# A spectral filter, soft mixture and gated layer on one core: the inverse basis multiplied straight into the spectrum, and expert weights loaded into the input's places

## Chip, core, metric

One core of one Trainium2 chip runs the whole kernel in one launch. The metric is device time in microseconds (us), the median of several runs. The kernel before takes 1540.72 us, the median of three runs (1538.58, 1540.72, 1543.03).

## What is computed

Three layers follow one another on 8 batches of 3072 tokens with 256 features each, all in float32.

```python
X = np.fft.rfft(x, axis=1)                       # x: (8, 3072, 256)
F = (filt_r + 1j * filt_i)[None, :, :]
y = np.fft.irfft(X * F, n=3072, axis=1).reshape(8 * 3072, 256)

logits = y @ phi                                 # 32 slots
d = softmax(logits, axis=0)                      # over all 24576 tokens
slot_input = d.T @ y                             # 32 x 256
slot_out = relu(slot_input @ w1[e]) @ w2[e]      # 8 experts, 4 slots each
z = softmax(logits, axis=1) @ slot_out

g = z @ w_gate
out = (silu(g) * (z @ w_val)) @ w_out            # 256 -> 1536 -> 256
```

## The kernel before

**First phase** (`phase1`). The kernel never transforms y back as a whole. It keeps the filtered spectrum in SBUF, since logits and slot inputs can both be had from it. The work is cut into 16 steps (8 batches, two halves `h` of 128 features), and a step into 6 units `u`. The loop over these 96 units writes the program in the order in which every engine runs it; nothing reorders it later.

- `s1_chunk` (lines 203 to 228) is the first stage of the Fourier transform: 4 chunks a step, each of 4 matmuls in four quadrants of the array (L217) into one PSUM tile `s`, a VectorE transpose to `sg` (L225), and a ScalarE copy to `b` (L234, in `spread`). It runs one step ahead of the units: in the usual plan one chunk in each of units 1 to 4.
- `s2_unit` (lines 239 to 271) is the second stage for one unit: 8 matmuls against the basis `fwd` (L248) into `X`, two VectorE products with the filter (P at L256, Q at L257), and two GpSimd combinations into `y` (L269, L271).
- `tr_unit` (lines 273 to 282) transposes `y` on TensorE against the identity (L279, 4 transposes a unit, two units later) and ScalarE copies the result (L281).
- `phi_pair` (lines 284 to 302), for every second unit, multiplies that by `phi` (L288) and gathers the slot logits' spectrum in `lts`.
- `chain` (lines 307 to 507) is a generator, one per batch, which `pump` advances by one step per unit while the next batch is under way. It transposes `lts` (L352), multiplies by the inverse basis `inv` (L362), transposes back (L372) and turns (L347) to the logits `lg`; takes the maximum (L397, L398), writes `lg` to memory (L402), forms exp(logit - max) (L420, L426), subtracts one (L430), transforms that forward again (L438, L450), puts the subtracted constant back at the zero frequency (L466), transposes (L471), and multiplies with `y` to the slot inputs of this batch (L481). Batch 6's chain is held back at step `HOLD` and interleaved with batch 7's behind the loop.
- `conv` (lines 558 to 597) reads 36 chunks of the three float64 weights `w_gate`, `w_val`, `w_out`, makes float32 out of their bits on VectorE (L584, L585, L591), ScalarE and GpSimd, and writes them back to memory. `first_weights` prepares the first batch's mixing weights. `aside` advances these two.

Loads are issued by SyncE, in program order: an issue that must wait for its place holds all issues behind it. `xp` holds two steps of x (16 KB of each partition for each), `bp` two steps of `b`, `sgp` the two `sg`. These, on the right side of SBUF, are given back behind the loop, and the first-layer expert weights `w1` (8 MB) go to their place (lines 714 to 718 and 758 to 762).

**Transition** (lines 731 to 871). `stage1` multiplies the slot inputs with `w1` (L783), `turn` transposes (L800), `stage2` multiplies with `w2` (L808, another 8 MB, in places that the first phase's tiles give back), and the result is multiplied with the gate and value weights (L843, L854).

**Second phase** (lines 940 to 1035). 576 items of 512 tokens by 128 hidden features: G and V (L959, L960), silu, product, split in two parts, and the output projection (L987, L991).

## Time and profile before

| | |
|---|---|
| median of three runs | 1540.72 us |
| the profiled execution | 1539.64 us, its span 1537.9 us |
| TensorE matmuls busy | 1449.9 us (94%) |
| VectorE busy | 1204.9 us (78%) |
| ScalarE busy | 955.1 us (62%) |
| GpSimd busy | 241.3 us (16%) |
| granted TensorE clock, mean | 0.991 |

The shares are averages over phases with different limits, so they are read by stage further down. "Busy" counts an engine from an instruction's start to its modelled end; a float32 matmul shows as two instructions, a transpose as one. "Idle before" gives the wait ahead of an instruction and what ended it. In the views by stretch the DMA share is the mean busy share of the core's 16 DMA engines.

### The profile page before, as it was taken

The page shows a single profiled execution, that of the slowest core. Times are in us where ns is not written, and L with a number is a line of the kernel's source. Part 1 is how long each engine was busy: PE and PEld are TensorE (multiplying, and loading weights), DVE is VectorE, ACT ScalarE, POOL GpSimd, SP SyncE. Part 2 cuts the span into 40 slices and gives each one's busy share as a digit, 9 for nine tenths or more (in the row PEclk, how much of TensorE's full clock was granted, in tenths as well). Part 3 has the DMA queues.
Part 4 walks back from the last instruction along what each step waited for, and adds up shares of the span by engine and source line. Part 5 has one row for each costly group of instructions (what it writes and reads, how often), then busy time and mean ns, then how long its engine had stood idle before and what let it go on. Part 6 is the DMA issues. An engine that isn't in the chain of part 4 may idle for free.

```text
span 1537.9 us, 26707 instructions
## 1 busy us (share of the span) xinstructions
PE 1449.9 (94%) x10282; PEld 1133.8 (74%) x10282; DVE 1204.9 (78%) x1976; ACT 955.1 (62%) x1808; POOL 241.3 (16%) x297
## 2 busy tenths in 40 slices
PE   3789998898869999999999999999999999999998
PEld 1455555555438888888888888888888888888887
DVE  3698899898328878887887788788778878877775
ACT  2365565564227666766766677677667667666665
POOL 1566555654010000000000000000000000000000
PEclk9999999999989999999999999999999999999999
DMA  9978678761990120121112013101301310120111
GB/s 193 189 132 147 115 132 142 124 117 56 366 279 25 35 68 19 29 69 27 27 35 71 16 28 69 30 23 35 72 15 29 69 35 18 35 62 14 28 29 28
DMA packets 90482, 116.53 MB, mean 76 GB/s; under 512 B 8657, under 2 KB 69970, under 8 KB 90034
## 3 DMA queue, kind: packets, MB, share of 16 engines
q1 hardware_dynamic: 88882, 111.15, 33.2%
q10 hardware_dynamic: 1216, 3.15, 1.1%
q8 instruction: 81, 1.33, 0.4%
q0 software_dynamic: 256, 0.52, 0.2%
q14 instruction: 47, 0.39, 0.1%
HBM read 68.13 MB, written 34.60 MB: 67 GB/s over the span
## 4 chain that ended last, share of the span: by engine, by line
PE 80%; DVE 11%; DMA 5%; issue 2%; ACT 1%; SPq 1%; POOL 0%; DVEq 0%; ACTq 0%; POOLq 0%
PE o L987 35%; PE o L991 18%; PE V L960 9%; PE G L959 9%; PE X L248 2%; DVE sg L225 2%; DVE P L256 2%; PE s L217 2%; DVE Q L257 2%; DMA fwd<-in_const_fwd_dram 2%; DMA raw<-in_moe_w_gate_dram 1%; PE T L279 1%; PE c L481 1%; DMA w<-in_moe_w_dram 1%; PE L L288 1%
## 5 line engine op out<-in xcount | busy, mean ns | idle before, releaser
L987 PE MATMUL o<-wo,hi 128*128 128x512 f32 x2304 | 831.1, 395 | 0.0
L991 PE MATMUL o<-wo,lo 128*128 128x256 f32 x2304 | 644.6, 280 | 0.2 <-DVE lo L976 0.2
L962 ACT ACTIVATE s<-G 128x512 f32<-128x512 f32 x576 | 344.7, 598 | 317.4 <-PE G L959 314.5
L968 DVE TENSOR_TENSOR h<-V,s 128x512 f32<-128x512 f32 x576 | 395.2, 686 | 168.9 <-ACT s L962 168.1
L987 PEld LDWEIGHTS o<-wo,hi 128*128 128x128 f32 x2304 | 432.0, 187 | 103.4
L991 PEld LDWEIGHTS o<-wo,lo 128*128 128x128 f32 x2304 | 433.6, 188 | 25.9 <-DVE lo L976 0.6
L976 DVE TENSOR_TENSOR lo<-h,hi 128x512 fp32r<-128x512 f32 x576 | 417.1, 724 | 0.1
L975 ACT CAST hi<-h 128x512 fp32r<-128x512 f32 x576 | 354.7, 616 | 12.5 <-DVE h L968 9.2
L960 PE MATMUL V<-c,v 128*128 128x512 f32 x576 | 227.4, 395 | 2.1 <-DVE h L968 1.8
L959 PE MATMUL G<-c,g 128*128 128x512 f32 x576 | 227.9, 396 | 0.0
L248 PEld LDWEIGHTS X<-b,fwd 128*64 128x64 f32 x1536 | 83.2, 138 | 67.9 <-issue 50.2
L959 PEld LDWEIGHTS G<-c,g 128*128 128x128 f32 x576 | 108.1, 188 | 25.6 <-issue 0.8
L234 ACT COPY b<-sg 128x768 f32<-128x768 f32 x64 | 58.7, 918 | 102.6 <-DVE sg L225 102.3
L225 DVE STREAM_TRANSPOSE sg<-s 128x1024 f32<-128x1024 f32 x64 | 78.9, 1236 | 47.9 <-PE s L217 47.9
L248 PE MATMUL X<-b,fwd 128*64 128x128 f32 x1536 | 106.3, 281 | 10.5 <-ACT b L234 5.0
L960 PEld LDWEIGHTS V<-c,v 128*128 128x128 f32 x576 | 108.6, 189 | 4.2 <-DVE h L968 2.9
L906 POOL TENSOR_TENSOR lg<-lg,mx 96x1024 f32<-96x1024 f32 x7 | 16.9, 2418 | 581.1 <-DVE mx L904 581.1
L217 PE MATMUL s<-x,csm 48*64 48x512 f32 x512 | 73.3, 628 | 34.2 <-DMA x<-in_x_dram 21.1
L1001 DVE TENSOR_TENSOR ot<-o,tmp 128x256 f32<-128x256 f32 x192 | 70.0, 423 | 39.5 <-ACT tmp L1000 39.5
L269 POOL TENSOR_TENSOR y<-P 128x256 f32<-128x256 f32 x96 | 70.2, 731 | 144.5 <-DVE P L256 144.5
L271 POOL TENSOR_TENSOR y<-Q 128x256 f32<-128x256 f32 x95 | 77.4, 815 | 0.9 <-DVE Q L259 0.8
L281 ACT COPY yt<-T 128x512 f32<-128x512 f32 x96 | 55.9, 582 | 30.4 <-PE T L279 29.9
(195 smaller groups left out, 1017.6 us busy)
## 6 DMA issues: line engine op xcount, KB each, us to landing
out_dram<-ot SPq DMA_DIRECT2D x192, 128.0 KB, 2.2
x<-in_x_dram SPq DMA_DIRECT2D x56, 384.0 KB, 8.2
w<-in_moe_w_dram SPq DMA_DIRECT2D x16, 1024.0 KB, 12.4
c<-ch SPq DMA_DIRECT2D x42, 128.0 KB, 2.4
c<-cl SPq DMA_DIRECT2D x42, 128.0 KB, 2.4
raw<-in_moe_w_gate_dram SPq DMA_DIRECT2D x12, 256.0 KB, 4.5
lgd<-lg SPq DMA_DIRECT2D x32, 96.0 KB, 6.9
raw<-in_moe_w_val_dram SPq DMA_DIRECT2D x12, 256.0 KB, 3.7
```

The lines of the kernel that those rows point to most:

```text
L217: pe.matmul(out=ps[64 * k:64 * k + 64, 16 * r:16 * r + 16, :], lhsT=s1t_sb[64 * r:64 * r + 48, :], rhs=xt[step][64 * r:64 * r + 48, k, :, ...
L225: dve.transpose(out=sg.rearrange("p j d k -> p d j k"), in_=ps.rearrange("p n d -> p d n"))
L248: pe.matmul(out=ps[par * 64:(par + 1) * 64, i, ri, :], lhsT=fwd[:, j, ri * 64:(ri + 1) * 64], rhs=bb[:, j, :],)
L271: eng.tensor_tensor(out=y[:, :, 1, :], in0=Q[:, :, 0, :], in1=Q[:, :, 1, :], op=ALU.add)
L959: pe.matmul(out=pg, lhsT=g4[c][:, fs], rhs=c4[b][:, q, G, :])
L960: pe.matmul(out=pv, lhsT=v4[c][:, fs], rhs=c4[b][:, q, G, :])
L962: act.activation(s, pg, AF.Silu)
L968: dve.tensor_tensor(out=h, in0=pv, in1=s, op=ALU.mult)
L975: act.copy(hi, h)
L976: dve.tensor_tensor(out=lo, in0=h, in1=hi, op=ALU.subtract)
L987: pe.matmul(out=a, lhsT=hi[:, ts], rhs=wo[f].rearrange("p k d -> p (k d)"), start=(f == 0), stop=(f == NF - 1), skip_group_check=True,)
L991: pe.matmul(out=a[:, D:2 * D], lhsT=lo[:, ts], rhs=wo[f][:, 0, :], start=False, stop=(f == NF - 1), skip_group_check=True,)
```

## The change

Five things are changed, all in the first phase and the transition.

1. `tr_unit` and its transposes go. `back_pair` takes their place: for two units together it multiplies the spectrum `y` (as the stationary operand, 64 rows at a time, the two halves of the array side by side) by the inverse basis `inv` (as the moving one): 16 matmuls into a PSUM tile of two banks, then one ScalarE copy of 1024 columns. The chain loses its first two steps (L352 as it was, and L362): it transposes `lts` once and turns it to logits. `inv` is needed from the first batch on, and is loaded ahead of the units. `phi_pair` now writes to the same PSUM tag as `back_pair`, which has one buffer.
2. The chain no longer subtracts one from the exponentials, nor puts the constant back. For all batches but the last, one reduction over both halves takes the place of two and their maximum.
3. Steps 2 and 3 (the second batch) get their x whole, in runs of 16 KB, in both x places, ahead of the units; step 4's load then has to wait until step 3's last chunk has read both. The first chunks of steps 3 and 4 move accordingly (`early`).
4. `w1` is loaded in pieces of 128 rows by 1024 columns into the places of x, `sg` and `b` as each comes free (behind units 83, 89, 90 and 95), so these pools stay until the transition has used them. The order of the `w2` loads changes.
5. The weight conversion starts four units later, and its last third (`w_out`) runs behind `first_weights`. The stores of `lg` of the last two batches are issued by ScalarE. `HOLD` is 5 in place of 8, in the shorter chain.

```diff
-HOLD = 8
+HOLD = 5
...
             def load_x(step, k):
                 b, h = divmod(step, 2)
-                if b >= NB:
+                if b >= NB or step == 3:
                     return
+                if step == 2:
+                    xt.setdefault(3, []).append(xp[k].tile([128, 16, D], F32, tag="x", name="x"))
+                    xt[2], ds = xt[3], slice(0, D)
+                else:
...
+            def expert_places(p, shape, tag, parts):
+                t = p.tile(shape, F32, tag=tag, name="w1")
+                for i, (e, d_) in enumerate(parts):
+                    w1s[e, d_] = t[:, i * FE:(i + 1) * FE] if len(shape) == 2 else t[:, i, :]
+                    nc.sync.dma_start(out=w1s[e, d_], in_=w1[e, 128 * d_:128 * d_ + 128, :])
...
-            def tr_unit(step, u):
...
-                        pe.transpose(out=ps[:, i, ri, :], in_=y[:, i, ri, :], identity=ident)
...
+            def back_pair(step, q):
+                b, h = divmod(step, 2)
+                ps = ps_t.tile([128, 2, 4, 128], F32, tag="T", name="T")
+                for g in range(4):
+                    y = yt[b, 2 * q + g // 2][:, g % 2]
                     for ri in range(2):
+                        for par in range(2):
+                            rows = slice(64 * par, 64 * par + 64)
+                            pe.matmul(
+                                out=ps[:, par, g, :],
+                                lhsT=y[rows, ri, h * 128:(h + 1) * 128],
+                                rhs=inv[rows, 2 * (4 * q + g) + ri, :],
+                                start=(ri == 0),
+                                stop=(ri == 1),
+                                tile_position=(64 * par, 0),
+                            )
+                t = ytp.tile([128, 2, 4, 128], F32, tag="yt", name="yt")
                 act.copy(t, ps)
...
             def phi_pair(step, q):
                 b, h = divmod(step, 2)
-                ps = ps_l.tile([128, 2, 2, 64], F32, tag="L", name="L")
+                ps = ps_t.tile([128, 2, 128], F32, tag="T", name="L")
...
-                lh = evac("lh", ps)
-                yield
-                ps = two()
-                for jj in range(NJ):
...
-                us = evac("us", ps)
-                yield
                 ps = small()
                 for k in range(6):
-                    pe.transpose(out=ps[:, k * 128:(k + 1) * 128], in_=col(us, k), identity=ident)
+                    pe.transpose(out=ps[:, k * 128:(k + 1) * 128], in_=lts[:, k // 2, k % 2], identity=ident)
...
-                for h in range(2):
-                    dve.tensor_scalar_add(dd[:, h], dd[:, h], -1.0)
...
-            side = [conv(), first_weights()]
+            side = [conv((0, 1)), first_weights(), conv((2,))]
...
+            early = [[], late, [[0], [1], [2], [3], [], []], [[], [], [0], [1], [2], [3]]]
...
+            at = [6 + p if p < 4 else 2 * p + 3 for p in range(len(units) // 2)]
+            behind = {a + 1: [p] for p, a in enumerate(at)}
...
             for i, (s, u) in enumerate(units):
-                if u in (0, 2):
+                if u in (0, 2) and s:
                     load_x(s + 2, u // 2)
-                if i == 6:
-                    nc.sync.dma_start(out=inv, in_=c_inv)
...
-                if i >= 8:
+                if i >= 12:
                     aside()
                 pump(1)
-                for c in plan[u] if s > 1 else late[u] if s else ():
+                for c in plan[u] if s > 3 else early[s][u] if s else ():
                     s1_chunk(s + 1, c)
...
+                if i == len(units) - 13:
+                    expert_places(xp[0], [128, 4, FE], "x", [(0, 0), (0, 1), (1, 0), (1, 1)])
+                if i == len(units) - 7:
+                    expert_places(xp[1], [128, 4, FE], "x", [(2, 0), (2, 1), (3, 0), (3, 1)])
+                if i == len(units) - 6:
+                    for d_ in range(2):
+                        expert_places(sgp, [128, FE], "sg", [(4, d_)])
+                    expert_places(bp[0], [128, 3, FE], "b", [(5, 0), (5, 1), (6, 0)])
...
-            cr.close()
-            for e in reversed(range(NEXP)):
-                w1s[e] = one([128, 2, FE], f"w1_{e}", c3, "right")
-            for e in range(4):
-                flat_load(w1s[e], w1[e], 128)
+            expert_places(bp[1], [128, 3, FE], "b", [(6, 1), (7, 0), (7, 1)])
...
-        for e in (4, 5):
-            flat_load(w1s[e], w1[e], 128)
-        flat_load(w2s[0], w2[0], 128)
-        for e in (6, 7):
-            flat_load(w1s[e], w1[e], 128)
         for e in (6, 7):
             flat_load(w2s[e], w2[e], 128)
         flat_load(wg, wd[0], 128)
-        for e in (1, 2, 3, 5, 4):
+        for e in (5, 0, 4, 1, 2, 3):
             flat_load(w2s[e], w2[e], 128)
         flat_load(wv, wd[1], 128)
```

**TensorE in a batch's stretch of the first phase.** The first rows are of the kernel before, three and a half units of the batch (X is a unit's second stage, T its transposes, L the product with phi, s the next step's first stage, c the chain; "x4" counts matmuls).

```order
L248 MATMUL X<-b,fwd 64x128 x8
L279 MATMUL T<-csm,y 128x128 x4
L288 MATMUL L<-yt,phi_sb 32x256 x4
L217 MATMUL s_1345<-x,csm 64x512 x4
L248 MATMUL X<-b,fwd 64x128 x8
L279 MATMUL T<-csm,y 128x128 x4
L352 MATMUL c<-csm,lts 128x128 x6
L217 MATMUL s_1391<-x,csm 64x512 x4
L248 MATMUL X<-b,fwd 64x128 x8
L279 MATMUL T<-csm,y 128x128 x4
L288 MATMUL L<-yt,phi_sb 32x256 x4
L362 MATMUL c<-inv,lha 32x128 x16
```

The same engine and place with the change (T is now the product with the inverse basis):

```order
L261 MATMUL X<-b,fwd 64x128 x8
L312 MATMUL L<-yt,phi_sb 32x256 x4
L230 MATMUL s_1320<-x,csm 64x512 x4
L261 MATMUL X<-b,fwd 64x128 x8
L295 MATMUL T<-inv,y 128x128 x16
L370 MATMUL c<-csm,lts 128x128 x6
L230 MATMUL s_1377<-x,csm 64x512 x4
L261 MATMUL X<-b,fwd 64x128 x8
L312 MATMUL L<-yt,phi_sb 32x256 x4
L387 MATMUL c<-t_1374,csm 64x512 x4
```

Units with 16 products and units with L now alternate, and the chain goes from its one transposition (L370) to the turned logits (L387) in the next unit.

**SyncE's issues behind the first batch's loads**, before (x of the second batch in pieces, `raw` the conversion's chunks, `wgd` its stores):

```order
L172 DMA x<-in_x_dram 48x16x128 x4
L570 DMA raw<-in_moe_w_gate_dram 128x512 x2
L172 DMA x<-in_x_dram 48x16x128 x2
L694 DMA inv<-in_const_inv_dram 128x3072
L172 DMA x<-in_x_dram 48x16x128 x2
L595 DMA wgd<-mn 128x256
```

and with the change:

```order
L645 DMA inv<-in_const_inv_dram 128x3072
L180 DMA x<-in_x_dram 48x4096 x4
L566 DMA raw<-in_moe_w_gate_dram 128x512 x2
L180 DMA x<-in_x_dram 48x16x128 x2
L591 DMA wgd<-mn 128x256
L566 DMA raw<-in_moe_w_gate_dram 128x512
```

The inverse basis and the second batch's whole x now stand ahead of the conversion. The third batch's first x load (the row with 48x16x128) stands ahead of the conversion's first store and of its third chunk.

## Rows read from the trace of the kernel before

**Rows 1.** Stretches, core 0: length, busy per engine, granted clock, DMA share, GB/s.
```profile
34.00:69.20 35.20, 25.50 (x300) 16.11 (x296) 24.62 (x41) 14.41 (x26) 20.48 (x29) 0.98 1.18 190
69.20:114.90 45.70, 40.83 (x481) 24.57 (x481) 40.80 (x68) 24.24 (x49) 24.45 (x33) 0.94 0.83 144
160.90:206.96 46.06, 41.75 (x534) 24.96 (x534) 42.12 (x71) 26.71 (x57) 27.02 (x37) 1.00 0.81 133
381.00:413.80 32.80, 24.43 (x336) 13.54 (x337) 16.17 (x41) 10.65 (x24) 3.06 (x5) 0.95 0.90 331
413.80:453.90 40.10, 27.20 (x236) 10.64 (x236) 5.57 (x9) 5.35 (x9) 0.00 (x0) 0.83 1.07 310
453.90:1537.90 1084.00, 1075.91 (x5764) 919.61 (x5760) 869.95 (x1414) 743.99 (x1385) 37.93 (x22) 1.00 0.16 38
```

**Rows 2.** Timeline of TensorE, one batch: the three waits, with the first-stage chunk.
```profile
188.61 0.27 PE L407 MATMUL c<-csm,cm 128*32 128x128 f32 x1 [1.01 <-DVE cm L398]
188.81 1.09 PE L217 MATMUL s<-x,csm 48*64 48x512 f32 x8
...
196.61 1.09 PE L217 MATMUL s<-x,csm 48*64 48x512 f32 x8 [1.57 <-DVE sg L225]
...
204.93 1.55 PE L450 MATMUL c<-fwd,bd 128*32 128x128 f32 x48 [1.04 <-DVE bd L347]
```

**Rows 3.** The same view: X, T and L of a unit, and the chain's transposes.
```profile
173.97 0.82 PE L352 MATMUL c<-csm,lts 128*128 128x128 f32 x6
...
182.72 1.09 PE L248 MATMUL X<-b,fwd 128*64 128x128 f32 x16
183.74 0.66 PE L279 MATMUL T<-csm,y 128*128 128x128 f32 x4
184.33 0.64 PE L288 MATMUL L<-yt,phi_sb 128*32 128x256 f32 x8
```

**Rows 4.** The chain of work that ended last, an inverse-basis step.
```profile
177.99 1.31 PE c L362 x48
```

**Rows 5.** Timeline of TensorE: two X in a row at the start; later units 6 and 12.
```profile
34.19 1.97 PE L248 MATMUL X<-b,fwd 128*64 128x128 f32 x32
...
47.09 1.09 PE L248 MATMUL X<-b,fwd 128*64 128x128 f32 x16
...
69.23 1.98 PE L248 MATMUL X<-b,fwd 128*64 128x128 f32 x16 [2.35 <-ACT b L234]
```

**Rows 6.** Timeline of TensorE's weight loads: the eight of one first-stage chunk.
```profile
188.81 0.21 PEld L217 LDWEIGHTS s<-x,csm 48*64 48x64 f32 x8
```

**Rows 7.** Groups of the first phase, shapes apart: weight loads of L217, copy of T.
```profile
L281 ACT COPY yt<-T 128x512 f32<-128x512 f32 x96 | 55.9, 582 | 30.4 <-PE T L279 29.9
...
L217 PEld LDWEIGHTS s<-x,csm 48*64 48x64 f32 x512 | 14.4, 134 | 61.0 <-DVE sg L225 27.3 <-issue 25.4 <-DMA x<-in_x_dram 4.8
```

**Rows 8.** Timeline of VectorE: the fourth unit's product; the subtraction of one.
```profile
44.14 0.69 DVE L256 TENSOR_TENSOR P<-X,ft 128x512 f32<-128x512 f32 x1 [4.12 <-issue]
...
198.15 1.83 DVE L430 TENSOR_SCALAR dd<-dd 128x512 f32<-128x512 f32 x2
```

**Rows 9.** Stretches again: whole x in flight; x in pieces in flight.
```profile
10.00:15.00 5.00, 0.00 (x0) 0.00 (x0) 0.00 (x0) 0.00 (x0) 0.00 (x0) 1.00 1.06 193
...
45.00:50.00 5.00, 4.52 (x62) 3.43 (x64) 4.48 (x8) 1.50 (x3) 4.82 (x8) 1.00 1.26 146
```

**Rows 10.** Timeline of TensorE: the last chain's start, and the transition's second stage.
```profile
387.36 1.03 PE L352 MATMUL cl<-csm,lts 128*128 128x128 f32 x6
...
390.91 0.66 PE L372 MATMUL c<-csm,usa 128*128 128x128 f32 x4 [0.33 <-ACT usa L334]
...
430.75 1.06 PE L808 MATMUL o<-w,ht 128*32 128x256 f32 x2 [8.03 <-DMA w<-in_moe_w_dram]
433.71 1.06 PE L808 MATMUL o<-w,ht 128*32 128x256 f32 x2 [1.90 <-DMA w<-in_moe_w_dram]
436.72 3.37 PE L808 MATMUL o<-w,ht 128*32 128x256 f32 x26 [1.95 <-DMA w<-in_moe_w_dram]
...
440.61 1.93 PE L808 MATMUL o<-w,ht 128*32 128x256 f32 x32
```

More of the change, by code (lines that the diff above doesn't have):

```diff
@@ L311, in two @@
                 def two(late=False):
-                    if late and b == NB - 2:
-                        return [p.tile([128, 512], F32, tag=t, name="cl") for p, t in ((ps_t, "T"), (ps_l, "L"))]
                     if not last:
-                        ps = small()
+                        ps = ps_t.tile([128, 1024], F32, tag="T", name="cl") if late and b == NB - 2 else small()
                         return [ps[:, 0:512], ps[:, 512:1024]]
@@ L324, in pair @@
                 def pair(name):
-                    if b == NB - 2 and name in ("dt", "dh"):
-                        return [ytp.tile([128, n], F32, tag="yt", name=name) for n in (512, 256)]
                     return [
@@ L382, in chain @@
                 else:
-                    lg = chp.tile([128, 2, E, 16], F32, tag="lg", name="lg")
-                    lg = [lg[:, h] for h in range(2)]
+                    both = chp.tile([128, 2, E, 16], F32, tag="lg", name="lg")
+                    lg = [both[:, h] for h in range(2)]
                 cm = chp.tile([128, 2, E], F32, tag="cm", name="cm")
@@ L426, in chain @@
                     act.activation(dd[:, h], dd[:, h], AF.Exp)
-                if not last:
-                    yield
-                for h in range(2):
-                    dve.tensor_scalar_add(dd[:, h], dd[:, h], -1.0)
                 yield
@@ L464, in chain @@
                     if q == 0:
[L465 to L467 removed]
+                        act.copy(sb_[:, b:b + 1], ps[0][0:32, 0:1])
                 yield
@@ L556, in flat, with conv @@
                 return a.rearrange("(p a) f -> p (a f)", p=128)
-            def conv():
+            def conv(kinds):
                 cw = 256
-                chunks = [(i, c) for i in range(3) for c in range(FF * D // 128 // cw)]
+                chunks = [(i, c) for i in kinds for c in range(FF * D // 128 // cw)]
                 raws = {}
@@ L648, in phase1 @@
                 load_filters(1)
+                nc.sync.dma_start(out=inv, in_=c_inv)
                 for step in range(2):
@@ L675, in pump @@
                 ready.clear()
+            at = [6 + p if p < 4 else 2 * p + 3 for p in range(len(units) // 2)]
+            behind = {a + 1: [p] for p, a in enumerate(at)}
             def tail_ops(i):
-                if 0 <= i - 2 < len(units):
-                    tr_unit(*units[i - 2])
-                if i - 4 >= 0 and i % 2 == 0 and i - 3 < len(units):
-                    s, u = units[i - 4]
-                    phi_pair(s, u // 2)
-                    if s % 2 == 1 and u == 4:
-                        ready.append((s // 2, chain(s // 2, s // 2 == NB - 1)))
+                for p in behind.get(i, ()):
+                    phi_pair(p // 3, p % 3)
+                    if p % 6 == 5:
+                        ready.append((p // 6, chain(p // 6, p // 6 == NB - 1)))
+                for p in (p for p in range(len(units) // 2) if at[p] == i):
+                    back_pair(p // 3, p % 3)
             def aside():
```

87 lines of the change are left out of this document (35 added, 52 removed).

## The prediction

> **What bounds the kernel now.** I read the time by stage first, because the shares on the page average over stages with different limits [rows 1]. From 453.9 us to the end the second phase keeps TensorE busy for 1075.9 of 1084.0 us, and the change touches none of its lines, so it costs nothing there. What can change is the 454 us ahead of it: the start (to unit 24, about 114.9), five even batches, the tail (to 413.8) and the transition (to 453.9).
>
> In an even batch (46.06 us) TensorE is busy for 41.75 us and VectorE for 42.12 [rows 1]: two engines near their limit, each of which now and then waits for the other. The timeline of TensorE shows where: 1.01 us for the maximum, 1.57 us for the transposes that free the only first-stage buffer, 1.04 us for the turn ahead of the forward transform [rows 2], 3.6 of the 4.3 us in which it stands. All three end with VectorE. At the start the DMA engines are full (share 1.18 from 34 to 69 us [rows 1]). In the transition, TensorE waits for expert weights at the second product, three times, 11.9 us in all [rows 10], and the granted clock averages 0.83 there [rows 1].
>
> **Even batches.** The new step has 16 matmuls of 128 columns for two units, shown as 32 instructions. Two X in a row take 1.97 us against 1.09 for one [rows 5]: 0.88 for sixteen instructions, 0.055 each, and 0.2 fixed. X also is 128 columns long and keeps two half arrays busy, split by columns where the new step splits by rows. At X's pace a pair costs 32 x 0.055 + 0.2 = 1.96 us. It takes the place of two T of 0.59 each (183.74 to 184.33 [rows 3]): +0.78 a pair, +4.7 a batch. The upper end is the pace of T, one transpose after another on the whole array: (0.59 - 0.2) / 4 = 0.10 each, so 3.4 us. I take 1.96, as the eight weight loads of a first-stage chunk, which go to four quarters of the array, end within 0.21 us [rows 6] where one of them takes 0.134 [rows 7]: loads into different row halves do run side by side. The Trainium skill, "TensorE: Matmul & The Clock Gate", section "LDWEIGHTS (loading the stationary operand)", speaks against the change: a load's time goes by its columns, and one of 32 rows takes as long as one of 128. One after another, by its formula (columns / 1.2 GHz, 107 ns for 128), the pair would take an estimated 3.6 us. The row above is what I go by.
>
> The chain loses the inverse basis step, 1.31 us [rows 4], and one of two groups of six transposes, 0.82 [rows 3]: -2.1. TensorE's work is then 41.75 + 4.7 - 2.1 = 44.35 us a batch. VectorE loses the subtraction, 1.83 us [rows 8], and two small instructions: 40.1 us. So TensorE becomes the only bound, and VectorE, 4 us behind it in work, should no longer make it wait much: between the logits' product and the maximum now lie a chunk, an X and often a full pair, about 4 us. I leave 0.7 us of waiting: 45.05 us, 1.0 less than now. From unit 24 to unit 86 are 62 / 12 = 5.2 batches: **-5 us**. Ends: no wait at all, -9; all 4.3 us kept, 48.65 us a batch, +13.5. ScalarE, with 26.7 of 46 us busy, hides its longer copy, and GpSimd's work stays.
>
> **The start.** Unit 6 starts at 47.1 and unit 12 at 69.2 [rows 5]. In units 6 to 9 there is now a pair in each, and L follows in the same single buffer, so each waits for the other's copy (0.58 us for half of T now [rows 7]). Unit 6: X 1.02 and T 1.96, with 0.5 for the inverse basis: 3.5. Units 7 and 8: 1.02 + 0.64 + 0.5 + 1.96, 4.1 each. Unit 9 the same plus a chunk of 1.02: 5.1. Unit 10: 2.7. Unit 11: X, T, two chunks and 1.3 between them: 6.3. Then the 2.35 us for the copy of b that unit 12 waits for today [rows 5]. Sum 28.1: unit 12 at 75.2. But unit 9's chunk needs the whole x of the second batch. It stands behind the filters, which the fourth unit's P waits for until 44.1 [rows 8], and behind the inverse basis (1.6 MB). At the 193 GB/s of the stretch in which the first batch's whole x is in flight [rows 9], 1.6 + 3.1 MB last 24 us: 65 to 68, where the chunk could run at 62.8. So unit 12 starts at about 78, +9.
>
> Behind it comes a wait that the change adds. Step 4's x goes where step 3's x still is until the end of unit 15, and SyncE holds its issue until then. Queued behind it are the conversion's first store and third chunk. That chunk's bytes follow 0.8 MB of x at about 146 GB/s [rows 9], 5.4 us, and land some 8 us after unit 15. VectorE meets the chunk in unit 16 and stands; TensorE has two X, an L and a pair to go before it needs the maximum behind that chunk: I put 5 us on the path. And as step 4's last chunk is made only in unit 23, unit 24 waits for b like unit 12: +2.4. From unit 12 to 24 that is 44.35 + 0.7 + 5 + 2.4 = 52.4 against 45.7 [rows 1]: +6.7. The start: **+15 us**; at least +7 (x in time, the chunk's wait covered), at most +18.
>
> **The tail.** The last chain starts with two steps fewer: 387.36 to 390.91 [rows 10], -3.5, and half of the subtraction, -0.5. Against that, the last pair with its longer copy adds 1.8, and the conversion's last third now falls on units 80 to 93, whose VectorE it had left: I put +1.2. Together **-1 us** (-5 to +3). The stores of the logits cost ScalarE issue time beside a wait for VectorE: nothing, 1 us if not hidden.
>
> **The transition.** w1 is in place before it. Behind unit 95 remain 1.6 MB of w1, 8.4 of w2 and 1.6 of the gate weights ahead of or among w2: 11.6 MB, where up to the second product there were 20 before. At 310 to 331 GB/s [rows 1] that is 35 to 37 us after 381, or 416 to 418; the second product starts near 422, a little earlier with the tail. So the three waits go, with the two pieces of 1.06 between them: 14.0 us. The clock too: 26 matmuls take 3.37 us behind the waits, 32 take 1.93 later [rows 10], so 1.8 more. That makes -15.8; I keep 1.3 for the last weights: **-14.5 us** (-16 to -6). Earlier loads run beside units 83 to 95, where the DMA engines are little used; their cover gone, they would show as waits of the first product.
>
> **Sum.** +15 - 5 - 1 - 14.5 = -5.5. The profiled execution took 1539.64 us (1.1 under the median): 1534.
>
> **Rivals.**
> *Weight loads of the two row halves don't overlap.* Then a pair takes 3.4 us, 1.44 more, on 48 pairs 69 us, nearly all on the path since TensorE is the bound: about 1600, slower. It decides early: from 2.1 us a pair on, the whole gain is gone. For it: no row here shows weights of 128 columns in two row halves; against it: rows 6. By the Trainium skill's page named above it would be 79 us more, an estimate. Chance 0.08.
> *TensorE keeps its waits*, because they come from the order of the program and not from VectorE's load: +13.5 for -5, so 1553, slower. For it: each wait ends with an instruction that stands in line behind other VectorE work. 0.13.
> *The start is nearly free* (+7): 1526. For it: the DMA engines carry 16 KB runs in place of 512 bytes. 0.25.
> *Loading w1 early doesn't do what it says*, since the waits shown are for w2, and w2's places come free no earlier; 6 us of wait stay: 1540, the same. 0.12.
>
> **How the numbers follow.** My forecast, 1534, has 0.42. About 0.3% (4.6 us) is what can be told from no change. Within the forecast's own spread I count 0.27 faster, 0.12 same, 0.03 slower; the free start is faster; the late w2 is mostly the same; the other two are slower (the kept waits with 0.02 as same). That gives 0.52, 0.25 and 0.23. The range reaches from the free start with no waits and 3 us more from the tail (1526 - 4 - 3 = 1519) to a start of 18 us with half of the waits kept (1534 + 3 + 9 = 1546), and leaves out the non-overlap and most of the kept waits.
>
> **What would show it.** Right: the pair's 32 instructions in about 2 us, an even batch near 45 us with TensorE over 97% busy, VectorE's wait for the third chunk behind unit 15, no wait of the second product over 1 us, w1 never waited for. Wrong: pairs of 3 us or more; a batch at 46 us or over; unit 24 before 122 us; waits for w2.

## The result, and the profile after

The changed kernel takes 1561.69 us, the median of four runs (1559.48 to 1567.1), beside 1541.88 us of the kernel before (four runs, 1538.58 to 1543.17): the ratio is 1.0137 with a 95% interval of 1.0103 to 1.0171. It is slower by some 20 us, and lies above the range of the prediction. The profiled span is 1562.1 us against 1537.9.

The start times of the first X of a unit (and of the first matmul of the transition's first product, and of the second phase), read from TensorE's timeline in us from the span's start, say where. The columns behind "after" are experiments below, by the first two characters of their labels.

| | before | after | r1 | r2 | r4 | f6 | g4 | g1 | h2 |
|---|---|---|---|---|---|---|---|---|---|
| unit 12 | 69.2 | 87.0 | 84.3 | 79.4 | 82.8 | 80.1 | 83.2 | 79.5 | 70.6 |
| unit 24 | 114.9 | 144.3 | 140.0 | 126.1 | 138.4 | 135.9 | 137.1 | 125.3 | 114.9 |
| unit 60 | 253.0 | 279.4 | 275.1 | 260.9 | 273.5 | 271.0 | 275.2 | 260.1 | 248.3 |
| unit 72 | 299.0 | 333.8 | 320.1 | 315.1 | 328.5 | 321.4 | 321.2 | 305.0 | 292.7 |
| unit 84 | 342.2 | 381.7 | 365.0 | 362.5 | 375.7 | 369.0 | 364.4 | 349.9 | 335.4 |
| unit 95 | 379.9 | 419.5 | 401.4 | 401.3 | 416.1 | 407.8 | 402.1 | 389.1 | 372.8 |
| transition | 413.8 | 454.1 | 440.5 | 433.6 | 447.1 | 451.1 | 435.0 | 422.3 | 408.6 |
| second phase | 453.9 | 478.2 | 493.0 | 457.8 | 485.3 | 475.2 | 476.8 | 446.4 | 438.0 |

To unit 24: +29.4. Units 24 to 60: 135.1 against 138.1, -3.0. Units 60 to 84: 102.3 against 89.2, **+13.1**. Unit 84 to the transition: +0.8. The transition: 24.1 against 40.1, -16.1. The sum, +24.2, is the difference of the spans. The medians differ by less: the profiled execution of after lies 2.2 us above the median of its four, and that of before 2.2 us below. Up to unit 24, after, r1, r4 and f6 run the same instructions, and the other three reach unit 24 at 135.9 to 140.0, so a start by itself varies by up to 8 us.

The stretches of after that answer to [rows 1]: start to unit 12, to unit 24, an even batch, the batches of units 60 to 72 and 72 to 84, and the transition (length, busy per engine, granted clock, DMA share, GB/s).

```profile
36.50:87.10 50.60, 35.15 (x422) 24.49 (x420) 22.54 (x35) 11.59 (x14) 16.82 (x24) 0.84 0.72 132
87.10:144.30 57.20, 48.53 (x625) 31.02 (x625) 38.44 (x65) 25.09 (x46) 27.23 (x36) 0.90 0.62 102
189.24:234.16 44.92, 43.94 (x627) 29.74 (x625) 38.70 (x66) 24.94 (x46) 27.63 (x37) 1.00 0.82 136
279.40:333.80 54.40, 46.90 (x627) 31.68 (x625) 40.33 (x64) 21.93 (x35) 24.12 (x30) 0.94 0.64 103
333.76:381.70 47.94, 44.76 (x626) 29.76 (x624) 36.58 (x66) 24.46 (x46) 26.16 (x37) 1.00 0.73 128
454.17:478.24 24.07, 23.06 (x237) 9.78 (x237) 5.64 (x9) 5.29 (x9) 0.00 (x0) 1.00 0.94 281
```

The even batch is as forecast: TensorE works 43.94 of 44.92 us, VectorE 38.70. The same work takes 54.40 us from unit 60 to 72 and 47.94 from 72 to 84, and the clock is down to 0.84 and 0.90 in the start, where before had 0.98 and 0.94. TensorE's timeline shows the places:

```profile
53.32 3.79 PE L295 MATMUL T<-inv,y 64*128 64x128 f32 x32 [3.83 <-DMA inv<-in_const_inv_dram]
...
72.86 1.07 PE L230 MATMUL s<-x,csm 48*64 48x512 f32 x2 [1.19 <-DMA x<-in_x_dram]
...
115.04 0.37 PE L409 MATMUL c<-csm,cm 128*32 128x128 f32 x1 [6.13 <-DVE cm L400]
...
207.42 2.06 PE L295 MATMUL T<-inv,y 64*128 64x128 f32 x32
209.40 0.29 PE L409 MATMUL c<-csm,cm 128*32 128x128 f32 x1
...
294.87 3.79 PE L295 MATMUL T<-inv,y 64*128 64x128 f32 x32 [5.49 <-DVE lts L324]
...
462.43 1.93 PE L807 MATMUL o<-w,ht 128*32 128x256 f32 x32
...
464.88 1.93 PE L807 MATMUL o<-w,ht 128*32 128x256 f32 x32
```

A product for two units (T) takes 2.0 us at the full clock (207.42 to 209.40) and 3.79 behind a wait, at the lower one. The maximum is no longer waited for (209.40, against 1.01 us in [rows 2]), nor is w2 (462.43, against [rows 10]). The two long waits, at 115 and 295 us, go back to VectorE, and from there to transfers:

```profile
113.27 0.29 DVE L580 TENSOR_SCALAR ex<-raw 128x256 int32<-128x256 int32 x1 [7.32 <-DMA raw<-in_moe_w_gate_dram]
...
292.20 1.00 DVE L607 TENSOR_REDUCE mx<-lgf 96x16 f32<-96x512 f32 x1 [5.06 <-DMA lgf<-lgd]
```

And SyncE's issues (time of issue, length) say why these are late:

```profile
38.94 3.01 SPq L180 DMA_DIRECT2D x<-in_x_dram  x4
42.64 1.24 SPq L566 DMA_DIRECT2D raw<-in_moe_w_gate_dram  x2
103.34 0.91 SPq L180 DMA_DIRECT2D x<-in_x_dram  x2
104.29 0.53 SPq L591 DMA_DIRECT2D wgd<-mn  x1
104.93 0.36 SPq L566 DMA_DIRECT2D raw<-in_moe_w_gate_dram  x1
...
283.27 0.40 SPq L603 DMA_DIRECT2D lgf<-lgd  x1
```

Nothing is issued from 43.9 to 103.3 us: step 4's x waits for its place, and the conversion's third chunk stands behind it, as predicted. The load of the first batch's logits (lgf) is issued at 283.27 and lands at 292.2, while `first_weights`, now in mid-phase at two steps a unit, wants it one unit behind.

### The profile page after: what moved, and what is told of

It is laid out like the page before. It is cut to its first block, busy times and chain, and to the rows that moved or that the text cites. A ratio compares the mean times of both kernels' runs of the same rounds, so it can differ in the third digit from the quotient of the medians.

```text
span 1562.1 us, 27951 instructions
## 1 busy us (share of the span) xinstructions
PE 1480.3 (95%) x11002; PEld 1178.0 (75%) x11002; DVE 1180.6 (76%) x1936; ACT 939.5 (60%) x1730; POOL 242.0 (15%) x297
## 4 chain that ended last, share of the span: by engine, by line
PE 83%; DVE 6%; DMA 6%; issue 1%; ACT 1%; POOL 1%; SPq 1%; DVEq 0%; ACTq 0%
PE o L986 34%; PE o L990 17%; PE V L959 9%; PE G L958 8%; PE T L295 4%; PE X L261 3%; PE s L230 2%; DMA x<-in_x_dram 2%; DVE sg L238 2%; DMA ft<-in_filt_r_dram 2%; PE c L477 1%; PE L L312 1%; DVE P L269 1%; DMA ft<-in_filt_i_dram 1%; DVE Q L270 1%
## 5 line engine op out<-in xcount | busy, mean ns | idle before, releaser
L261 PEld LDWEIGHTS X<-b,fwd 128*64 128x64 f32 x1536 | 85.1, 140 | 67.4 <-issue 53.6
L295 PE MATMUL T<-inv,y 64*128 64x128 f32 x1536 | 103.3, 286 | 15.0 <-DVE lts L324 8.4
L295 PEld LDWEIGHTS T<-inv,y 64*128 64x128 f32 x1536 | 94.1, 195 | 25.0 <-issue 12.8
L230 PE MATMUL s<-x,csm 48*64 48x512 f32 x512 | 77.1, 645 | 26.7 <-DMA x<-in_x_dram 24.3
```

The lines of the kernel that those rows point to most:

```text
L230: pe.matmul(out=ps[64 * k:64 * k + 64, 16 * r:16 * r + 16, :], lhsT=s1t_sb[64 * r:64 * r + 48, :], rhs=xt[step][k][64 * r:64 * r + 48, :, ...
L261: pe.matmul(out=ps[par * 64:(par + 1) * 64, i, ri, :], lhsT=fwd[:, j, ri * 64:(ri + 1) * 64], rhs=bb[:, j, :],)
L295: pe.matmul(out=ps[:, par, g, :], lhsT=y[rows, ri, h * 128:(h + 1) * 128], rhs=inv[rows, 2 * (4 * q + g) + ri, :], start=(ri == 0), stop=( ...
```

## The experiments

Ratios are to runs of the kernel before on the same chip (medians of 1540.3, 1543.3, 1542.3 and 1542.4 us in the four groups of runs: r, f, g and h). Times of different groups, and of after, are set against one another below as they are; as before's own median moves by 3 us among the groups, such a difference is uncertain by about as much.

### r1_order: the side work as before

```diff
-            side = [conv((0, 1)), first_weights(), conv((2,))]
+            side = [conv((0, 1, 2)), first_weights()]
...
-                if i == 10 or i >= 12:
+                if i == 10 or i >= 12 and (len(side) > 1 or i >= len(units) - 4):
```

> The changed kernel, but conversion and first batch's weights in the order and at the pace of before (all 36 chunks, then first_weights at one step a unit). Theory 1 (first_weights in mid-phase makes VectorE, and so TensorE, wait for its load of the logits): units 60 to 72 fall from 54.4 to about 46 us, units 72 to 86 by about 2.7, and some of it comes back in units 84 to 95; about 1551 us against 1561.7. Rival (these units are slow because of the pairs' own work or the rising VectorE load, whatever stands there): within 2 us of 1561.7.

Measured: 1578.17 us, ratio 1.0245 (1.0219 to 1.0271), slower still. Units 60 to 72 did fall to 44.9 us, and units 60 to 84 to 89.9 against 102.3. But the conversion starts four units later than in before, so the last step of `first_weights` falls behind the loop, where its VectorE instruction stands behind the last chains. Its store holds SyncE's queue, and w2 behind it; the waits of SyncE (us in total, times, longest) and TensorE's second product:

```profile
SPq L626 <- DVE ctf L624: 27.7, 2, 26.6
```
```profile
462.99 1.03 PE L807 MATMUL o<-w,ht 128*32 128x256 f32 x2 [14.13 <-DMA w<-in_moe_w_dram]
```

The theory held for the units that it named and failed in the time. So the mid-phase place is a cost, and the new order also had a use: it keeps the side work's end off w1 and w2.

### r2_pieces: the second batch's x in halves, as before

```diff
-                if step == 2:
-                    xt.setdefault(3, []).append(xp[k].tile([128, 16, D], F32, tag="x", name="x"))
...
-            load_x(2, 0)
-            load_x(2, 1)
...
-            early = [[], late, [[0], [1], [2], [3], [], []], [[], [], [0], [1], [2], [3]]]
+            early = [[], late, plan, plan]
```

> The changed kernel, but the second batch's x in halves of the features as before, and the first stage's chunks in the usual plan; the inverse basis still ahead of the units. Theory 2 (the start is lost to the order of transfers: 3.1 MB of x whole, on which unit 9's chunk waits and which hold the queue for step 4's x): unit 12 starts near 76 us in place of 87, unit 24 near 128 in place of 144; about 1546 us. Rival (the start is lost to the pairs and to the inverse basis, which is ahead in both): unit 24 falls by less than 5 us; about 1558 us.

Measured: 1544.24 us, ratio 1.0027 (1.0015 to 1.0039): 17.5 us below after. Unit 24 starts at 126.1. Units 60 to 72 still take 54.28. The theory of the start holds, and the size is right within 2 us.

### r3_unheld: step 4's x issued when its place is free

```diff
-                if u in (0, 2) and s:
-                    load_x(s + 2, u // 2)
+                if s and (u in (4, 5) if s == 2 else u in (0, 2)):
+                    load_x(s + 2, u // 2 if s != 2 else u - 4)
```

> The changed kernel, but step 4's x is issued in units 16 and 17, when its place is free, in place of units 12 and 14, so that it holds nothing behind it. Theory 2b (the held queue leaves the DMA engines idle from 74 to 103 us and costs the wait for the conversion's third chunk): unit 24 comes 6 to 8 us sooner, about 1555 us. Rival (the queue costs nothing, as the conversion would wait anyway for its first chunks behind x): within 2 us of 1561.7.

Measured: 1558.8 us, ratio 1.0113 (1.0093 to 1.0133), some 3 us below after, with intervals that overlap (after's is 1.0103 to 1.0171). Units 12 to 24 take 56.7 us against 57.2, and unit 24 starts at 140.7, within what the same code shows in after, r1, r4 and f6 (135.9 to 144.3); the 6 to 8 us that I had expected did not come. The wait for the chunk is gone, and another stands in its place. SyncE's issues, VectorE and TensorE of this kernel:

```profile
101.85 3.17 SPq L180 DMA_DIRECT2D x<-in_x_dram  x4
105.12 5.18 SPq L404 DMA_DIRECT2D lgd<-lg  x4
```
```profile
117.33 1.31 DVE L365 STREAM_TRANSPOSE bd<-c 128x512 f32<-128x512 f32 x2 [5.51 <-DMA lgd<-lg]
```
```profile
118.79 2.80 PE L448 MATMUL c<-fwd,bd 128*32 128x128 f32 x48 [5.28 <-DVE bd L365]
```

The stores of the logits now stand behind step 4's x, and `bd` takes the buffer that they free. Mending the held queue alone does not help: all of x, conversion and stores falls due in these units, and whichever is last is waited for.

### r4_w1late: w1 where before loaded it

```diff
-                if i == len(units) - 13:
-                    expert_places(xp[0], [128, 4, FE], "x", [(0, 0), (0, 1), (1, 0), (1, 1)])
...
+            cr.close()
...
+            for e in range(4):
+                flat_load(w1s[e], w1[e], 128)
```

> The changed kernel, but the w1 of the experts loaded where and in the order before loaded them, and w2 in the order of before. Theory 3 (early w1 takes the waits for w2 away and costs the first phase nothing): the transition is back at 40 us, 16 longer, units 83 to 95 unchanged; about 1577 us. Rival (the early loads collide with units 83 to 95): these units get 2 to 5 us shorter, about 1573 to 1575 us.

Measured: 1573.84 us, ratio 1.0212 (1.019 to 1.0234), 12.2 above after. The transition takes 38.2 us against 24.1, and units 84 to 95 do not get shorter (40.3 against 37.8). Early w1 is worth 14 us in the transition, and nothing shows that it costs the first phase anything in this order of the side work.

### f6_yields and f7_both: the load of the logits two steps earlier

```diff
                     nc.sync.dma_start(out=lg, in_=lgd[0][:, G])
-                    yield
-                    yield
+                    for _ in range(4):
+                        yield
```

> The changed kernel, but the first batch's weights wait four steps (two units) in place of two (one unit) behind the issue of their load of the logits; nothing else moves. Theory 1, sharpened by r1_order (units 60 to 72 were back at 44.9 us there, but the end of first_weights then stood behind the tail and held the queue): it is this one load, 8.9 us from issue to landing, that VectorE meets too early; its 5.06 us wait and TensorE's 5.49 us go, and the lower clock behind them: units 60 to 72 at 45 to 46 us, about 1553 us against 1561.7. Rival (the wait moves on to the second load or to another one behind it, as a wait moved in r3_unheld): units 60 to 84 shorter by less than 3 us, 1559 us or more.

Measured: 1563.55 us, ratio 1.0147 (1.0119 to 1.0174): no gain. Units 60 to 72 fell to 50.4 us, and units 60 to 84 from 102.3 to 98.0; VectorE still waits for the load, 2.4 us. But the conversion now ends two units later (95 in place of 93), and there its last chunk is issued behind nine loads of w1. VectorE meets it, and TensorE waits for VectorE:

```profile
399.95 4.68 SPq L187 DMA_DIRECT2D w<-in_moe_w_dram  x9
405.94 0.33 SPq L591 DMA_DIRECT2D wod<-mn  x1
407.25 0.33 SPq L566 DMA_DIRECT2D raw<-in_moe_w_out_dram  x1
```
```profile
416.35 0.29 DVE L580 TENSOR_SCALAR ex<-raw 128x256 int32<-128x256 int32 x1 [10.77 <-DMA raw<-in_moe_w_out_dram]
```
```profile
418.52 3.45 PE L295 MATMUL T<-inv,y 64*128 64x128 f32 x32 [9.63 <-DVE lts L324]
```

> The changed kernel with the second batch's x in halves of the features (as in r2_pieces) and the four steps behind the load of the logits. If the two costs are apart and add up: 1544.2 of r2_pieces less 8.5, about 1536 us, below before's 1540 to 1542. Rival (the waits are exchanged for one another): 1542 us or more.

Measured: 1551.65 us, ratio 1.0053 (1.0034 to 1.0071), where r2_pieces had 1.0027, with the same wait at the end (8.77 us). The rival held in f7_both. In f6_yields its time and its moved wait came, while units 60 to 84 got shorter by 4.3 us, more than the 3 that it allowed.

### f8_spread: the first products later

```diff
-            at = [6 + p if p < 4 else 2 * p + 3 for p in range(len(units) // 2)]
+            at = [9 + p if p < 7 else 2 * p + 3 for p in range(len(units) // 2)]
```

> As f7_both, but the first seven products with the inverse basis stand in units 9 to 15 in place of 6 to 11, 13 and 15. Theory (what is left of the start's loss, some 11 us by unit 24, is four products in a row, each waiting for the copy of the one ahead, the first two at the lower clock): unit 12 sooner by 4 us or more, unit 24 by about 3; about 3 us below f7_both. Rival (the work is merely moved, and TensorE is the bound up to unit 24): unit 24 within 1 us of f7_both.

Measured: 1563.96 us, ratio 1.0144 (1.0123 to 1.0164), 12 us above f7_both. My theory fell, and its rival too: it is worse. Unit 9 starts at 53.6 (f7_both: 60.1), but unit 16 at 108.9 (f7_both: 92.2). The products now stand among the chunks of steps 2 and 3, TensorE waits 0.6 to 1.5 us for ScalarE or VectorE ahead of each product from 66 to 106 us, and in the gaps the granted clock falls (the third column from the end of the stretches). These rows show where the time goes; what of it is the waits' and what the clock's was not taken apart:

```profile
60.00:70.00 10.00, 8.02 (x55) 5.22 (x57) 2.54 (x3) 1.26 (x2) 1.41 (x2) 0.55 0.94 141
70.00:80.00 10.00, 7.41 (x87) 3.98 (x84) 3.67 (x4) 4.01 (x5) 1.41 (x2) 0.94 0.01 4
80.00:90.00 10.00, 7.07 (x62) 5.38 (x60) 3.22 (x6) 1.32 (x3) 1.64 (x2) 0.57 0.57 80
```

### f10_w1late: f7_both without the early w1

The edit is that of r4_w1late on top of f7_both.

> As f7_both, but w1 loaded where before loaded it: of the five parts of the change only the product with the inverse basis, the shorter chain and the missing subtraction are left, with the small moves. By r4_w1late the early w1 is worth 12 to 14 us; so f7_both plus 12 to 14, about 1549 us, slower than before by 8. Rival (with the other two costs gone the product by itself wins): at or below before.

Measured: 1557.87 us, ratio 1.0096 (1.0078 to 1.0114), 6 above f7_both, where I had expected 12 to 14, and 9 above the forecast of 1549 us: the transition is 18.7 us longer, but the wait of 8.77 us goes with the w1 loads that caused it. The second product waits again:

```profile
449.46 1.06 PE L803 MATMUL o<-w,ht 128*32 128x256 f32 x2 [9.41 <-DMA w<-in_moe_w_dram]
```

### g1_three: three parts undone

r2_pieces, with the side work in before's order, at its pace and from unit 8 as in before. Against r2_pieces, order, pace and place of the side work thus change together:

```diff
-            side = [conv((0, 1)), first_weights(), conv((2,))]
+            side = [conv((0, 1, 2)), first_weights()]
...
-                if i >= 12:
+                if i >= 8:
                     aside()
...
-                if i == 10 or i >= 12:
+                if i == 4 or i >= 8 and (len(side) > 1 or i >= len(units) - 4):
                     aside()
```

> The changed kernel with three things as before: the second batch's x in halves of the features, the conversion from unit 8 and all of it ahead of first_weights, and first_weights at one step a unit. What stays of the change: the product with the inverse basis, the shorter chain, no subtraction, w1 into the places of x, sg and b. Theory (both losses come from the reordered side work and from the whole x, not from the product; in f6 and f7 and in r1_order the end of the side work ran into w1's loads or past the loop, and with four units more it no longer does): unit 24 near 124 to 126, units 24 to 84 at 45 us a batch, the tail as in r2_pieces, the transition 24 us: about 1530 us, faster than before by 10. Rival (side work at the old place meets w1's loads on SyncE's queue again): a wait of VectorE of 5 us or more behind unit 84, 1538 us or more.

Measured: **1531.09 us, ratio 0.993 (0.9914 to 0.9946)**, faster than before by 11 us and than after by 30. Its stretches (start, to unit 24, an even batch, transition) and TensorE in units 5 to 7:

```profile
34.70:79.50 44.80, 31.38 (x422) 23.34 (x418) 24.80 (x41) 13.58 (x20) 20.12 (x28) 0.92 1.03 169
79.50:125.30 45.80, 45.33 (x625) 30.63 (x625) 38.59 (x65) 23.91 (x45) 25.53 (x34) 0.96 0.76 126
170.26:215.18 44.92, 43.94 (x627) 29.73 (x625) 38.70 (x66) 24.95 (x46) 27.63 (x37) 1.00 0.79 136
...
422.33:446.41 24.08, 23.07 (x237) 9.78 (x237) 5.64 (x9) 5.29 (x9) 0.00 (x0) 1.00 0.90 268
```
```profile
46.84 3.68 PE L256 MATMUL X<-b,fwd 128*64 128x128 f32 x32 [5.08 <-DVE Q L265]
...
50.94 2.54 PE L290 MATMUL T<-inv,y 64*128 64x128 f32 x32 [0.43 <-DMA inv<-in_const_inv_dram]
...
55.80 2.06 PE L290 MATMUL T<-inv,y 64*128 64x128 f32 x32 [0.58 <-ACT lts L317]
```

Against before: start +10.4, units 24 to 84 -2.7, the tail +0.8, the transition -16.1; together -7.6 of the -7.9 between the spans.

### g2_minus_one: g1_three with the subtraction

```diff
                     act.activation(dd[:, h], dd[:, h], AF.Exp)
+                for h in range(2):
+                    dve.tensor_scalar_add(dd[:, h], dd[:, h], -1.0)
                 yield
...
-                        act.copy(sb_[:, b:b + 1], ps[0][0:32, 0:1])
+                        zero = dt_[0][0:32, 0:1]
+                        dve.tensor_scalar_add(zero, zero, float(SEQ))
+                        act.copy(sb_[:, b:b + 1], zero)
```

> As g1_three, but with the subtraction of one (two VectorE instructions a batch, 1.83 us) and the constant put back. Theory (VectorE is 6 us behind TensorE's work in a batch, so its work has cover): even batches within 0.3 us of g1_three, the time within 3 us. Rival (the chain's instructions stand in line on VectorE and each delays TensorE by its length): 1.8 us a batch, 12 us or so in all.

Measured: 1536.85 us (before: 0.9966, 0.9954 to 0.9977), 5.8 above g1_three; I had expected at most 3. A batch takes 45.39 us, 0.47 more (five of them 2.4), and unit 84 to the transition 3.9 more, where the last two chains run with little beside them. The 1.83 us of a batch are hidden to three quarters here, and not in the tail.

### g3_before_side: the side work's new order in the kernel before

```diff
-            side = [conv(), first_weights()]
+            side = [conv((0, 1)), first_weights(), conv((2,))]
...
-                if i == 4 or i >= 8 and (len(side) > 1 or i >= len(units) - 4):
+                if i == 4 or i >= 8:
```

> The kernel before with one part of the change: the conversion's last third behind first_weights, all at two steps a unit. Theory 1 (the order itself makes VectorE meet the load of the logits one unit behind its issue, whatever TensorE does): about 8 us are lost in the 12 units around first_weights (units 56 to 68), the time 1546 to 1550 us. Rival (it costs only where the products are, since TensorE has no slack there): within 2 us of before.

Measured: 1542.65 us, ratio 0.9999 (0.999 to 1.0009): the same. The wait is there, 3.28 us on VectorE and 4.05 on TensorE, but units 48 to 72 are only 3.0 us longer (95.0 against 92.1), and units 72 to 84, where part of the conversion now stands, another 1.8. This execution is the longest of its ten, and in the medians nothing of it is left:

```profile
250.29 1.00 DVE L611 TENSOR_REDUCE mx<-lgf 96x16 f32<-96x512 f32 x1 [3.28 <-DMA lgf<-lgd]
```
```profile
254.18 2.70 PE L450 MATMUL c<-fwd,bd 128*32 128x128 f32 x48 [4.05 <-DVE bd L347]
```

So the order costs 12.5 us in its units with the product, and by itself some 5 there, and nothing that can be told from the whole time. The rival's reason, that TensorE has no slack beside the products, fits; but the wait on VectorE is also shorter here (3.28 us against 5.06), so the reason isn't shown apart from that.

### g4_before_whole: the second batch's x whole in the kernel before

The edit makes `load_x`, the slices of x and the first chunks (`early`) those of the change; all else is before's.

```diff
+            load_x(2, 0)
+            load_x(2, 1)
+            early = [[], late, [[0], [1], [2], [3], [], []], [[], [], [0], [1], [2], [3]]]
...
-                if u in (0, 2):
+                if u in (0, 2) and s:
                     load_x(s + 2, u // 2)
```

> The kernel before with one part of the change: the second batch's x whole, ahead of the units, with the first chunks moved as the change moves them. Theory 2 (the whole x by itself costs the start): r2_pieces gave 17.5 us for undoing it in the changed kernel; without the inverse basis ahead of it x lands some 8 us sooner, so 8 to 12 us are lost by unit 24; about 1550 us. Rival (it costs only behind the inverse basis): unit 24 within 3 us of 114.9.

Measured: 1561.45 us, ratio 1.0123 (1.011 to 1.0136), 19 us slower by this part alone; unit 24 starts at 137.1, +22.2. The chain of waits, TensorE's timeline and VectorE's:

```profile
43.00 25.61 DMA x<-in_x_dram
```
```profile
68.65 1.96 PE L220 MATMUL s<-x,csm 48*64 48x512 f32 x2 [4.34 <-DMA x<-in_x_dram]
```
```profile
107.53 0.29 DVE L587 TENSOR_SCALAR ex<-raw 128x256 int32<-128x256 int32 x1 [6.93 <-DMA raw<-in_moe_w_gate_dram]
```

The product has no part in it: unit 9's chunk waits for all 256 features of x where its step needs 128, and the held queue brings the late chunk of the conversion with it.

### h1_before_w1 and h2_before_w1_nosub: without the product

The kernel before with the early w1, then also without the subtraction. The first edit is `expert_places` and its four calls as in the change, its order of w2, and

```diff
-            cr.close()
-            for e in reversed(range(NEXP)):
...
+            expert_places(bp[1], [128, 3, FE], "b", [(6, 1), (7, 0), (7, 1)])
...
-                        nc.sync.dma_start(
+                        (nc.scalar if b >= NB - 2 else nc.sync).dma_start(
```

> The kernel before with one part of the change: w1 into the places of x, sg and b, the change's order of the w2 loads, and the last two batches' stores of the logits issued by ScalarE. Theory 3 (the early w1 is worth its 12 to 14 us by itself): about 1528 us. Rival (in before, the longer chain's tail and the side work's end at unit 95 leave it less): 1533 us or more.

Measured: 1531.43 us, ratio 0.9928 (0.9911 to 0.9944): 11 us by the early w1 (with its order of w2 and the stores on ScalarE), near the theory. The transition takes 28.8 us here, 11.4 less than in before, where after has 16.1 less. The other 4.7 us go with a wait for w2 and the lower clock behind it, which this kernel and the next still show. SyncE holds w2's loads until a slot-input product of the last chains (L487) has read the place: 10.2 us here, where the longest such wait in g1_three is 3.4 us. SyncE's wait in this kernel (total, times, longest), and TensorE's second product:

```profile
SPq L128 <- PE cl L487: 10.2, 1, 10.2
```
```profile
427.38 3.54 PE L813 MATMUL o<-w,ht 128*32 128x256 f32 x26 [2.33 <-DMA w<-in_moe_w_dram]
```

So the last 5 us of the transition's gain come with the rest of the change, under which w2's places are free sooner; the product, the shorter chain and the smaller `HOLD` were not tried apart in this.

```diff
-                    dve.tensor_scalar_add(dd[:, h], dd[:, h], -1.0)
...
-                        zero = dt_[0][0:32, 0:1]
-                        dve.tensor_scalar_add(zero, zero, float(SEQ))
-                        act.copy(sb_[:, b:b + 1], zero)
+                        act.copy(sb_[:, b:b + 1], ps[0][0:32, 0:1])
```

> As h1_before_w1, and without the subtraction of one. Theory 4 (the product with the inverse basis by itself is a loss of some 7 us: 10 at the start, and half of the gain of the batches is the missing subtraction's): about 1524 us, faster than g1_three by 7. Rival (the product is what makes VectorE's work cheap; with the transposes the engines wait for one another as before): 1531 us or more, no faster than g1_three.

Measured: **1520.02 us, ratio 0.9856 (0.984 to 0.9873)**, the fastest of all: 22 us below before, 11 below g1_three, 42 below after. The missing subtraction alone is worth 11.4 us here by the medians. The two profiled executions differ by 5.8 us only, as that of h1_before_w1 is the shortest of its four and this one, at 1524.45 us, the longest; units 24 to 84 take 6.8 us less, and where the rest of the 11.4 lies isn't shown. An even batch of this kernel, in the stretches:

```profile
159.58:203.96 44.38, 41.23 (x535) 24.85 (x535) 40.32 (x68) 26.60 (x57) 26.81 (x37) 1.00 0.77 138
```

With the transposes TensorE still waits for 3.15 us of a batch, and the batch is 0.54 us shorter than g1_three's, where it works 43.94 and waits for 1.

### h3_before_inv: only the inverse basis ahead

```diff
+                nc.sync.dma_start(out=inv, in_=c_inv)
                 for step in range(2):
...
-                if i == 6:
-                    nc.sync.dma_start(out=inv, in_=c_inv)
```

> The kernel before with one part of the change: the inverse basis loaded ahead of the units in place of unit 6. Theory 4 (the start's remaining +10 are TensorE's four products in units 6 to 9, with copies and the lower clock): unit 24 within 2 us of 114.9, 1542 us. Rival (it is the 1.6 MB ahead of the second batch's x): unit 24 later by 5 us or more, 1547 us.

Measured: 1545.15 us, ratio 1.0019 (1.0009 to 1.0028): 2.7 us by the medians. In the profiled execution, at 1549.5 us the longest of its ten, unit 24 comes 7.2 us later, and unit 9's chunk waits for x:

```profile
62.36 1.96 PE L217 MATMUL s<-x,csm 48*64 48x512 f32 x2 [1.22 <-DMA x<-in_x_dram]
```

The rival holds in the profile, and the medians lie between the two: of the 10 us that g1_three loses at the start some 3 to 7 are the transfer's, an estimate, and what is left I put down to the products by subtraction.

## Why the prediction was wrong

**The start, +15, was the first failed step**: it measured +29.4 in the profile, and +21 to +29 over the four kernels with the same code up to unit 24, past its upper end of +18. The mechanisms were right and their terms too small. "1.6 + 3.1 MB last 24 us: 65 to 68" rested on 193 GB/s, but x landed at 72.9, and while it was in flight all transfers together moved 173 GB/s:

```profile
43.90:73.00 29.10, 19.62 (x239) 15.39 (x240) 9.21 (x15) 5.16 (x7) 9.81 (x14) 0.82 0.95 173
```

And no term stood for the clock, which fell behind these waits, so that T took 3.79 us for 2.0. I charged the whole x with some 10 us (3 to unit 12, 5 for the third chunk, 2.4 for b). Undoing it gave 17.5 (r2_pieces), doing it alone cost 19 (g4_before_whole). What the product and the early inverse basis cost the start without it is +10.4 (g1_three), where my working had +6.

**The second failed step was one left out.** "The conversion's last third now falls on units 80 to 93" looked at where the conversion goes and not at what takes its place: `first_weights` in units 60 to 70, at twice the pace, with a load that it meets one unit after the issue. The new order cost 12.5 us there (units 60 to 84: 102.3 in after, 89.9 in r1_order). How much of that is this one load's stays open: a further unit of distance took back 4.3 us (f6_yields), with 2.4 us of VectorE's wait left. Before's rows could not show the wait; that VectorE would meet the load sooner stood in the order of the program, and I had costed VectorE's work there, not its waits.

**The even batches, -5, were right per batch, for the wrong reason, and wrong in number.** The product took 2.0 us for 1.96, the batch 44.9 for 45.05. But I let VectorE's relief pay for the product. Taken apart, the relief alone brings the batch to 44.4 (h2_before_w1_nosub), and the product then puts back what it adds to TensorE: the 2.6 us of work that I had worked out eat TensorE's last waits and 0.5 more. And I multiplied one batch's gain by 5.2, though before's batch of units 72 to 84 already took 43.15 us, as its conversion ended there (in unit 79); with the product it takes 44.9. This stretch in before:

```profile
299.02:342.17 43.15, 41.23 (x534) 24.83 (x534) 39.21 (x66) 24.68 (x51) 25.31 (x35) 1.00 0.71 126
```

So g1_three gains 2.7 where I had 5, and h2 gains 6.8.

**The transition, -14.5, was right in size** (-16.1), and the granted clock rose from 0.83 to 1.00 as forecast. But I gave all of it to the early w1, which by itself brings 11.4 (h1_before_w1); the rest needs w2's places sooner, and my working counted w2's bytes and no wait for a place. **The tail, -1**, measured +0.8, inside its bounds.

Of the rivals none came: the weight loads overlap, TensorE's waits in a batch went, the start was not free, w2 was not late in after (in h1_before_w1, without the product and the shorter chain, it was). Every sign that I named as "right" appeared, down to VectorE's wait for the third chunk (7.32 us), and the sum was wrong all the same. The signs tested the terms that I had, not the one that I lacked; that one shows only in a sign of "wrong", a batch at 46 us or over (54.4 and 47.9 from unit 60 to 84).

By parts, then, in medians: early w1 -11 (h1), no subtraction -11 (h2), the product with the inverse basis, the shorter chain, `HOLD` and the early load of the basis together some +11 (g1_three against h2; in the profiles +10.4 to unit 24, +4.1 to unit 84, -0.8 to the transition and -5.3 in it), the whole x +17 to +19 (r2, g4), and the side work's order some +13 behind the product (r2_pieces against g1_three) and nothing without (g3). Their sum is +19 to +21, and +20 was measured. With +17 for the whole x these are steps of one chain of kernels from before to after, so they must add up, and the agreement proves nothing; g3, g4, h1 and h3 are parts tried alone.

## What to carry to other kernels

Take a change apart: two of its parts alone were 22 us faster than before, all together 20 slower. When a part leaves an engine without slack, ask of everything that is reordered how far ahead of its use each load is issued: an order that left the time as it was in before (g3) cost 12.5 us here. And waits behind one in-order issue queue are exchanged rather than removed when one of them is mended (r3_unheld and f6_yields each brought up the next, and r1_order's moved side work held w2).

## What was not expected of the hardware

Weight loads into the two row halves overlap, as the four quarters of [rows 6] had let me expect. The group of after's even batch (busy in us, mean ns of one):

```profile
L295 PEld LDWEIGHTS T<-inv,y 64*128 64x128 f32 x192 | 11.2, 188 | 1.5 <-POOL y L282 0.7 <-issue 0.5 <-POOL y L284 0.2
```

192 loads of 188 ns would be 36 us one after another, and they fill 11.2. The Trainium skill ("TensorE: Matmul & The Clock Gate", "LDWEIGHTS (loading the stationary operand)") has a load's time go by its columns whatever its rows. That loads come one at a time, which gave the estimate of 3.6 us a pair, was my addition to it, and the measured 2.0 decides against that.

A wait cost more than its length here: TensorE's 5.49 us at 294.87 were followed by a product of 3.79 us in place of 2.0. Units 60 to 72, with a granted clock of 0.94, lost 9.5 us against r1_order; TensorE was busy for 46.9 us in them in place of 43.95, so some 3 of the 9.5 are work at the lower clock, and the rest waits.
